# Twelve VectorE operations in other places of a hand-listed order, and seven PSUM tiles in other banks

## The chip, the cores and the metric

One core of one Trainium2 chip. The metric is the device time of one execution in microseconds (us); the number for a kernel is the median of its runs. Before the change: 225.25 us, three runs from 223.98 to 225.33.

## The reference

For x of 2048 rows by 640 columns (bf16) the kernel computes `g * A + (1 - g) * B`. The gate `g` is a sigmoid of a weighted row sum of x. Branch A is a long convolution: `kv = shift(k) * v` with four taps, then a convolution along the 2048 rows with a 2048-long kernel per column, then a product with q (= x).

```python
k_shift = k_shift + k_pad[:, t:t + S, :] * shift_k[:, ks - 1 - t]     # four taps
kv = k_shift * v
y_f = rfft(kv padded) * rfft(ssm_k padded)
a = q * (irfft(y_f)[:S] + kv * ssm_D)
```

Branch B is a mixer: layernorm, a 640x640 matmul and gelu, four column groups of the result shifted by +1, -1, +2 and -2 rows, a second 640x640 matmul and a residual add, then layernorm, 640x1536, gelu, 1536x640 and a residual.

```python
h = gelu(layernorm(x) @ w1)                      # then four groups of 160 columns shifted in rows
x1 = x + shifted(h) @ w2
b = x1 + gelu(layernorm(x1) @ w3) @ w4
```

## The kernel before

The kernel first records 1176 operations (`Prog.op`, `Prog.dma`), each with the memory that it reads and writes, and then issues them in one global order written out by hand, the list `SEQUENCE`. `schedule` follows that list and gives every PSUM tile the bank that the list `PLACES` holds for it. `emit` splits the order by engine (320 operations on TensorE, 299 on ScalarE, 401 on VectorE, 53 on GpSimd, 103 DMAs on SyncE) and puts semaphore waits where the recorded memory use needs them. So an engine runs its own operations strictly in the listed order, and an operation whose input is late holds up all that stand behind it on its engine. A PSUM tile's first matmul also waits for whoever read the earlier tile in the same bank.

Most operations are recorded by a few helpers, so that nearly all of VectorE's rows in the profile have line L646 (`tt`, a tensor_tensor), nearly all of ScalarE's L656 (`act`), nearly all of TensorE's L678 (`mm`) and the DMAs L234 or L237. Operations are told apart by their shapes, their places and their numbers in `SEQUENCE`.

Branch A works on column chunks c = 0 to 4 of 128 columns. For each: `h_*` transforms the convolution kernel, `kv` applies the taps and the product with v (ScalarE scales, VectorE adds), `kv2`, `x_fwd` and `combine` transform kv, `unit` multiplies the two transforms block by block, and `final` transforms back and multiplies by q. The `unit` is the largest VectorE part; it is what the text calls a product unit:

```python
def unit(c):                       # L1003, shortened
    for o0 in (2, 0):              # two halves of the output blocks
        for a in range(o0 + 2):
            for i in range(2):     # acc[i] for a = 0, else the scratch tmp[i]
                tt(tmp[i] if a else acc[i], x[...], HF[:, c, a, i]..., ALU.mult)
            for i in range(2 if a else 0):
                if turn(...): P.dma("pool", acc[i], tmp[i], accum=True)   # an adding DMA
                else: tt(acc[i], acc[i], tmp[i], ALU.add)
        tt(Y[:, :, 0], ...); tt(Y[:, :, 1], ...)          # result back into XF
        scale(Y[0:1, ...])                                # first row, ScalarE or VectorE
```

Some of the additions are thus adding DMAs that GpSimd issues (L237, GpSimd's queue) after VectorE's products; the next product into the same scratch buffer has to wait for the DMA to land. In unit 0 the products 632 and 633 fill acc[0] and acc[1], 634 and 635 fill tmp[0] and tmp[1], 636 adds tmp[0], 637 is the adding DMA of tmp[1] into acc[1], and 639 is the next product into tmp[1]. Unit 3 has the same pattern with DMA 768 and product 770.

Branch B's matmuls are `mm1`, `mm2` (its result is added to x by VectorE, L966), `mm3` (12 groups of 5 matmuls of 128x512 for each quarter of the rows, gelu by ScalarE) and `mm4`. TensorE's list interleaves them with branch A's transforms; the last of `mm4`, operation 977 of tile 14, stands ahead of most of the last `final`s. The `final`s of column group 1 add branch B's result and store.

In `mm1` the fifth column tile goes through a buffer and is copied, 32 partitions at a time, to shifted places of `hT` (line L932, or by DMA); these copies start at odd or even columns.

Of the kernel before, what the change touches and what calls it, by code (L numbers as in the profile page):

```python
# [433 lines left out]
def bass_gated_mix__ssm_conv_h3__mixer_s_mlp__prompt_kernel(  # L434
    nc, A_q, A_k, A_v, A_shift_k, A_ssm_k, A_ssm_D, B_x, B_w1, B_w2, B_w3, B_w4, gate_w, out,
):
    S, D, F = 2048, 640, 1536
# [3 lines left out]
    P = Prog(nc)  # L441
# [27 lines left out]
    def ps(n, cls):  # L469
# [3 lines left out]
    SEQUENCE = [2, 4, 27, 1, 24, 7, 0, 5, 3, 8, 46, 53, 9, 10, 11, 45, 52, 12, 13, 14, 49, 15, 50, 16, 17, 25, 18,  # L473
# [207 lines left out]
    sp = "sp"  # L681
# [233 lines left out]
    def mm1(sc, t0, n, parts=range(5)):  # L915
        xt = chunk_of[0, sc]
        i0 = t0 // 128 % 4
        for ft in parts:
# [5 lines left out]
            else:  # L924
                hx = hxb[t0 // 256 % 2][:, 0:n]
                act(hx, pr, ACTF.Gelu_apprx_tanh)
                for g in range(4):
                    c0, q = 2 + SHIFT[g] + t0, slice(32 * g, 32 * (g + 1))
                    if turn(sc > 0):
                        P.dma(sp, hT[q, 4, c0:c0 + n], hx[q, :], after=[hT[q, 4, c0 - 1:c0]])  # L930
                        continue
# [135 lines left out]
    for sc in range(4):  # L1067
# [8 lines left out]
        else:  # L1076
            n = 256 if sc < 2 else 512
# [72 lines left out]
```

## Time and profile before

| | |
|---|---|
| Median of three runs | 225.25 us (223.98 to 225.33) |
| Profiled execution: span from first to last instruction | 222.3 us |
| The profiled execution's own time | not told beside its span; the median is 2.95 us above the span |
| Granted TensorE clock, mean | 0.993 |
| TensorE busy | 210.2 us (95%) |
| VectorE busy | 211.8 us (95%) |
| ScalarE busy | 193.4 us (87%) |
| Last VectorE operation, by the timeline | ends at 219.55 us |

Engine names in the rows: PE is TensorE's matmuls, PEld its weight loads, DVE is VectorE, ACT is ScalarE, POOL is GpSimd, SP is SyncE. A row of a timeline gives start, length, engine, line, operation, shapes and count, and in brackets the idle time ahead of it and what ended it. Neighbouring operations of one line are merged into one row, under the shape of the first.

### The profile page before, as it was taken

The numbers are of one execution on the slowest core, as the hardware profiler recorded it, in microseconds if no ns is written. First come the engines' busy times: TensorE is split into PE (matmuls) and PEld (weight loads), VectorE is DVE, ScalarE is ACT, GpSimd is POOL, SyncE is SP. The second block draws the span as 40 slices with busy tenths as digits, with TensorE's granted clock in tenths as the row PEclk, the third lists the DMA queues.
The fourth block names the chain that finished last, engine by engine and source line by source line (L and its number), as shares of the span: only waits on it lengthen the run. The fifth ranks groups of instructions, "written<-read, shape, count | busy, mean of one in ns | idle before, by whom it ended". The sixth has DMA issues, their size and how long they took to land.

```text
span 222.3 us, 3842 instructions
## 1 busy us (share of the span) xinstructions
PE 210.2 (95%) x1403; PEld 125.7 (57%) x1410; DVE 211.8 (95%) x417; ACT 193.4 (87%) x324; POOL 53.5 (24%) x57
## 2 busy tenths in 40 slices
PE   5999989799999999999999999999999999999971
PEld 2588755344675444665445575445666444677650
DVE  6999999899999979999999999999998999999994
ACT  2389999799999999899999999999987698666891
POOL 0422303200003300005140003034015416287431
PEclk9999999999999999999999999999999999999997
DMA  5997999999999999939958874599699959979895
GB/s 166 344 299 181 213 208 246 169 253 190 147 361 212 321 226 172 200 78 189 233 108 146 200 153 94 119 174 184 142 226 138 232 77 265 200 100 96 110 161 112
DMA packets 80561, 41.39 MB, mean 186 GB/s; under 512 B 59129, under 2 KB 77086, under 8 KB 80542
## 3 DMA queue, kind: packets, MB, share of 16 engines
q1 hardware_dynamic: 73872, 31.89, 64.9%
q0 software_dynamic: 6496, 9.18, 26.7%
q8 instruction: 11, 0.18, 0.3%
q10 hardware_dynamic: 174, 0.07, 0.1%
q14 instruction: 8, 0.07, 0.1%
HBM read 14.88 MB, written 5.77 MB: 93 GB/s over the span
## 4 chain that ended last, share of the span: by engine, by line
DVE 65%; PE 13%; ACT 11%; DMA 7%; issue 2%; ACTq 0%
DVE arena L646 59%; ACT arena L656 11%; PE PSall L678 10%; DMA arena<-arena 7%; PE PSall L701 3%; DVE arena L651 2%; DVE arena L932 1%; DVE arena L847 1%; DVE arena L966 1%; PE PSall L908 0%; DVE arena L852 0%; DVE arena L698 0%; DVE arena L848 0%; PE PSall L731 0%; DVE arena L689 0%
## 5 line engine op out<-in xcount | busy, mean ns | idle before, releaser
L678 PE MATMUL PSall<-arena 128*128 128x512 bf16 (+5 forms) x1342 | 202.0, 309 | 4.9 <-DVE arena L646 2.2
L646 DVE TENSOR_TENSOR arena<-arena 128x1024 bf16<-128x1024 bf16 (+13 forms) x266 | 173.4, 712 | 4.1 <-DMA arena<-arena 2.7
L678 PEld LDWEIGHTS PSall<-arena 128*128 128x128 bf16 x1349 | 121.4, 98 | 85.1 <-ACT arena L656 6.7
L656 ACT ACTIVATE arena<-PSall 128x512 bf16<-128x512 f32 (+6 forms) x157 | 93.4, 666 | 10.7 <-PE PSall L736 4.9
L656 ACT ACTIVATE arena<-arena 128x640 bf16<-128x640 bf16 (+5 forms) x105 | 90.7, 892 | 4.5 <-DVE arena L646 4.2
L855 POOL TENSOR_TENSOR arena<-arena 128x2 f32<-128x2 f32 (+2 forms) x15 | 17.1, 1145 | 87.6 <-DVE arena L852 71.4
L237 POOL DMA_DIRECT2D out_dram<-arena x24 | 25.5, 1285 | 15.1 <-DVE arena L646 8.9
L656 ACT ACTIVATE arena<-PSall,arena 128x640 bf16<-128x640 f32 (+2 forms) x32 | 20.4, 655 | 8.5 <-PE PSall L678 8.4
L237 POOL DMA_DIRECT2D arena<-arena x14 | 12.4, 882 | 61.1 <-DVE arena L646 61.1
L966 DVE SCALAR_TENSOR_TENSOR arena<-PSall,arena 128x640 bf16<-128x640 f32 x16 | 12.9, 814 | 0.5 <-PE PSall L678 0.5
L651 DVE TENSOR_SCALAR arena<-arena 128x640 bf16<-128x640 bf16 (+6 forms) x37 | 13.2, 376 | 0.1
L847 DVE BATCH_NORM_STATS2 arena<-arena 128x6 f32<-128x320 bf16 x20 | 8.8, 479 | 1.1 <-DMA arena<-in_A_q_dram 1.0
L701 PE MATMUL PSall<-arena 128*128 128x512 bf16 x15 | 6.4, 586 | 2.2 <-DVE arena L698 2.2
L932 DVE TENSOR_SCALAR arena<-arena 32x256 bf16<-32x256 bf16 (+1 forms) x23 | 5.5, 237 | 0.6 <-ACT arena L656 0.3
L656 ACT ACTIVATION_READ_ACCUMULATOR arena<-arena 128x1 f32 x28 | 5.8, 206 | 0.0
L701 PEld LDWEIGHTS PSall<-arena 128*128 128x128 bf16 x15 | 1.9, 136 | 5.0 <-issue 2.8
L908 PE MATMUL PSall<-arena 128*128 128x128 bf16 x40 | 3.4, 220 | 0.1
L852 DVE SCALAR_TENSOR_TENSOR arena<-arena 128x2 f32<-128x2 f32 (+2 forms) x19 | 3.0, 157 | 0.2 <-ACT arena L656 0.2
L908 PEld LDWEIGHTS PSall<-arena 128*128 128x128 bf16 x40 | 2.5, 98 | 0.5 <-DVE arena L651 0.2
L704 ACT ACT_TABLE_LOAD x1 | 1.3, 1283 | 1.3 <-PEq L1135 1.3
L848 DVE BATCH_NORM_AGGREGATE arena<-arena 128x2 f32<-128x12 f32 x10 | 1.8, 199 | 0.0
L966 DVE DVE_READ_ACCUMULATOR arena<-PSall,arena 128x1 f32 x16 | 1.3, 79 | 0.0
(19 smaller groups left out, 2.9 us busy)
## 6 DMA issues: line engine op xcount, KB each, us to landing
arena<-arena POOLq DMA_DIRECT2D x9, 512.0 KB, 6.5
arena<-in_A_ssm_k_dram SPq DMA_DIRECT2D x5, 512.0 KB, 4.2
arena<-in_A_q_dram SPq DMA_DIRECT2D x6, 320.0 KB, 5.7
arena<-in_B_w_dram SPq DMA_DIRECT2D x1, 1920.0 KB, 10.5
out_dram<-arena SPq DMA_DIRECT2D x16, 96.0 KB, 2.9
out_dram<-arena POOLq DMA_DIRECT2D x16, 96.0 KB, 4.7
arena<-in_A_q_dram SPq DMA_DIRECT2D x8, 192.0 KB, 3.3
out_dram<-arena POOLq DMA_DIRECT2D x8, 192.0 KB, 4.2
```

What stands on the lines that cost most here:

```text
L237: fn = lambda e: e.dma_start(out, in_, **kw)
L646: P.op(eng, lambda e: e.tensor_tensor(o, real(a), real(b), op), [a, b], [o], dve_ns(o, [a, b], 2) if eng == "dve" else 500)
L651: P.op(eng, lambda e: e.tensor_scalar(o, real(a), s1, s2, op0=op0, **({} if op1 is None else {"op1": op1})), [a] + aps, [o], dve_ns(o, [a] ...
L656: P.op("act", lambda e: e.activation(real(o), real(a), f, bias=bias, scale=scale, **({"accum_out": accum} if accum is not None else {})), ...
L678: fns.append(lambda e, l=l, r=r, i=i: e.matmul(real(o), l, r, start=(i == 0), stop=(i == last)))
L701: P.op("pe", lambda e: e.matmul(real(pw), warm[:, 0:128], warm[:, 128:640], start=True, stop=True), [warm], [pw], 427.0 if i < 14 else 216.0)
L847: P.op("dve", lambda e, o=o, i=i: e.bn_stats(o, i), [i], [o], 400)
L852: P.op("dve", lambda e: e.scalar_tensor_tensor(o, a, x, b, op0=op0, op1=op1), [a, b] + aps, [o], n_of(o) / 0.96 + 65)
L855: P.op("pool", lambda g: g.tensor_tensor(o, a, e, ALU.pow), [a, e], [o], dur)
L908: P.op("pe", [lambda e, c=c, pb=pb, xn=xn: e.transpose(real(pb)[:, 128 * c:128 * (c + 1)], xn[:, 128 * c:128 * (c + 1)], ident) for c in r ...
L932: P.op("dve", lambda e, o=hT[q, 4, c0:c0 + n], i=hx[q, :]: e.tensor_scalar(o, i, 1.0, None, op0=ALU.mult), [hx[q, :]], [hT[q, 4, c0:c0 + n ...
L966: P.op("dve", lambda e: e.scalar_tensor_tensor(x, real(pr), 1.0, x, op0=ALU.mult, op1=ALU.add, accum_out=st[1, 0][:, t:t + 1]), [pr, x], [ ...
```

## The change

Read by engine, the new `SEQUENCE` leaves the order of TensorE, ScalarE, GpSimd and SyncE as it was. On VectorE twelve operations of 401 stand elsewhere:

| Operation | What it is | Place before | Place now |
|---|---|---|---|
| 633 | unit 0, first half, product into acc[1] | 168 | 159 |
| 389 | combine(1), the second half (subtract) | 204 | 179 |
| 678 | unit 1, second half, product into tmp[1] | 238 | 232 |
| 677 | unit 1, second half, product into tmp[0] | 243 | 238 |
| 693 | h_even(4), the difference | 287 | 278 |
| 701 | kv(4), the first add of shifted taps | 260 | 266 |
| 766 | unit 3, first half, product into tmp[0] | 290 | 288 |
| 770 | unit 3, first half, product into tmp[0] behind DMA 768 | 305 | 307 |
| 814 | unit 4, second half, result Y part 1 | 353 | 356 |
| 815 | unit 4, second half, the first row | 357 | 360 |
| 1166 | last final (group 1, o 0, q 1), the sum | 388 | 383 |
| 1170 | the same final, product with q, first tile | 395 | 389 |

One wait on another engine's queue follows: GpSimd's DMA 637 waits for both products 633 and 635; the later of the two was 633 and is now 635.

VectorE where unit 0 begins, before. L966 rows are `mm2`'s adds (tiles 13, 8 and 11 in the first row, then 15, 12 and 14), the single 128x2048 row is product 632, the 128x2047 row is add 407 of kv(2), and the three 128x2048 rows are products 635, 634 and 633.

```order
L966 SCALAR_TENSOR_TENSOR arena<-PSall,arena 128x640 x3
L852 SCALAR_TENSOR_TENSOR arena<-arena 128x4
L646 TENSOR_TENSOR arena<-arena 128x2048
L966 SCALAR_TENSOR_TENSOR arena<-PSall,arena 128x640
L646 TENSOR_TENSOR arena<-arena 128x2047
L966 SCALAR_TENSOR_TENSOR arena<-PSall,arena 128x640
L852 SCALAR_TENSOR_TENSOR arena<-arena 128x4
L646 TENSOR_TENSOR arena<-arena 128x2048 x3
L966 SCALAR_TENSOR_TENSOR arena<-PSall,arena 128x640
```

The same place now (a line is added ahead, so L966 reads L967):

```order
L967 SCALAR_TENSOR_TENSOR arena<-PSall,arena 128x640 x2
L646 TENSOR_TENSOR arena<-arena 128x2048
L967 SCALAR_TENSOR_TENSOR arena<-PSall,arena 128x640
L852 SCALAR_TENSOR_TENSOR arena<-arena 128x4
L646 TENSOR_TENSOR arena<-arena 128x2048
L967 SCALAR_TENSOR_TENSOR arena<-PSall,arena 128x640
L646 TENSOR_TENSOR arena<-arena 128x2047
L967 SCALAR_TENSOR_TENSOR arena<-PSall,arena 128x640
L852 SCALAR_TENSOR_TENSOR arena<-arena 128x4
L646 TENSOR_TENSOR arena<-arena 128x2048 x2
L967 SCALAR_TENSOR_TENSOR arena<-PSall,arena 128x640
```

Product 633 was the last of the three 128x2048 rows and now stands ahead of the add of mm2(11), operation 564.

VectorE a little later, before: the add 410 of kv(2) (128x2047), kv2(1), the add 411 (128x2046), and the product 639 that waits for DMA 637.

```order
L646 TENSOR_TENSOR arena<-arena 128x1024 x2
L646 TENSOR_TENSOR arena<-arena 128x2047
L646 TENSOR_TENSOR arena<-arena 128x1024
L646 TENSOR_TENSOR arena<-arena 128x2046
L646 TENSOR_TENSOR arena<-arena 128x2048
```

The same place now:

```order
L646 TENSOR_TENSOR arena<-arena 128x1024 x2
L646 TENSOR_TENSOR arena<-arena 128x2047
L646 TENSOR_TENSOR arena<-arena 128x1024
L646 TENSOR_TENSOR arena<-arena 128x3x2x256
L646 TENSOR_TENSOR arena<-arena 128x2046
L646 TENSOR_TENSOR arena<-arena 128x2048
```

The 128x3x2x256 row is 389, which came 25 operations later, ahead of unit 1's product 661.

VectorE at the end of unit 4, before: 812 and 811 (128x1024), 814 (128x2x512), 1103 of a final (128x256), 813, 1104, 815 (one row).

```order
L646 TENSOR_TENSOR arena<-arena 128x1024 x2
L646 TENSOR_TENSOR arena<-arena 128x2x512
L646 TENSOR_TENSOR arena<-arena 128x256
L646 TENSOR_TENSOR arena<-arena 128x2x512
L646 TENSOR_TENSOR arena<-arena 128x256
L651 TENSOR_SCALAR arena<-arena 1x2x2x128
L646 TENSOR_TENSOR arena<-arena 128x384
```

The same place now:

```order
L646 TENSOR_TENSOR arena<-arena 128x1024 x2
L646 TENSOR_TENSOR arena<-arena 128x256
L646 TENSOR_TENSOR arena<-arena 128x2x512
L646 TENSOR_TENSOR arena<-arena 128x256
L646 TENSOR_TENSOR arena<-arena 128x2x512
L646 TENSOR_TENSOR arena<-arena 128x384
L646 TENSOR_TENSOR arena<-arena 128x256
L646 TENSOR_TENSOR arena<-arena 128x384
L651 TENSOR_SCALAR arena<-arena 1x2x2x128
```

1103 and 1104 each move one result ahead of unit 4's, and the first row 815 comes three operations later.

In `PLACES` seven tiles get other banks: tile 66 (x_fwd(1), first quarter) 4 to 6, tiles 123 and 125 (mm4(1), mm4(3)) 4 to 6 and 6 to 4, tile 134 (mm3(1)) 6 to 3, tiles 142, 143 and 148 (mm3(2)) 4 to 6, 2 to 4 and 4 to 2. With them the waits of some matmuls for ScalarE's reads of earlier tiles go to other reads; the one that comes to wait for a later read with the least in hand is 890, the first matmul group of mm3(2), which waited for 870 and now waits for 895.

The third part is in `mm1`: a shifted copy that starts at an odd column now also waits for the copy that wrote the column beside it, and the two memsets at the edges are recorded as two columns wide.

```diff
-    SEQUENCE = [2, 4, 27, 1, 24, 7, 0, 5, 3, 8, 46, 53, ...
+    SEQUENCE = [27, 46, 2, 4, 1, 7, 45, 0, 5, 24, 3, 8, ...
...
-    P.op("dve", lambda e: e.memset(hT[0:32, 4, 2:3], 0.0), [], [hT[0:32, 4, 2:3]], 70)
+    P.op("dve", lambda e: e.memset(hT[0:32, 4, 2:3], 0.0), [], [hT[0:32, 4, 2:4]], 70)
...
-    P.op("dve", lambda e: e.memset(hT[32:64, 4, S + 1:S + 2], 0.0), [], [hT[32:64, 4, S + 1:S + 2]], 70)
+    P.op("dve", lambda e: e.memset(hT[32:64, 4, S + 1:S + 2], 0.0), [], [hT[32:64, 4, S:S + 2]], 70)
...
                     c0, q = 2 + SHIFT[g] + t0, slice(32 * g, 32 * (g + 1))
+                    near = [hT[q, 4, c0 - 1:c0]] if c0 % 2 else []
                     if turn(sc > 0):
-                        P.dma(sp, hT[q, 4, c0:c0 + n], hx[q, :], after=[hT[q, 4, c0 - 1:c0]])
+                        P.dma(sp, hT[q, 4, c0:c0 + n], hx[q, :], after=near)
                         continue
                     P.op("dve", lambda e, o=hT[q, 4, c0:c0 + n], i=hx[q, :]: e.tensor_scalar(o, i, 1.0, None, op0=ALU.mult),
-                         [hx[q, :]], [hT[q, 4, c0:c0 + n]], n / 3.84 + 65)
+                         [hx[q, :], *near], [hT[q, 4, c0:c0 + n]], n / 3.84 + 65)
```

This gives three copies (122, 184 and 185) a wait for an earlier copy on VectorE itself.

More of the change, by code (lines that the diff above doesn't have):

```diff
@@ L471, in ps @@
         return v if n == 1 else v.rearrange("p (b n) -> p b n", b=2)
-    SEQUENCE = [2, 4, 27, 1, 24, 7, 0, 5, 3, 8, 46, 53, 9, 10, 11, 45, 52, 12, 13, 14, 49, 15, 50, 16, 17, 25, 18,
[59 rows of a table removed]
-    PLACES = [2, 4, 7, 0, 4, 5, 6, 1, 2, 1, 3, 4, 2, 3, 3, 4, 2, 6, 7, 2, 0, 4, 5, 7, 6, 2, 6, 1, 0, 7, 4, 1, 6, 0,
[6 rows of a table removed]
+    SEQUENCE = [27, 46, 2, 4, 1, 7, 45, 0, 5, 24, 3, 8, 47, 25, 48, 28, 9, 130, 26, 10, 11, 31, 53, 12, 52, 32, 13,
[59 rows of a table added]
+    PLACES = [2, 4, 7, 0, 4, 5, 6, 1, 2, 1, 3, 4, 2, 3, 3, 4, 2, 6, 7, 2, 0, 4, 5, 7, 6, 2, 6, 1, 0, 7, 4, 1, 6, 0,
[6 rows of a table added]
     ON = ("0000000011111111111111111011011100110100010000101111000000000000011000000000110100000001010010001101"
```

130 rows, old and new, of tables (PLACES, SEQUENCE) are left out of this document.

## The prediction

> **What bounds the kernel now.** I read the busy line of the page first, then the chain of waits in order of time, then the busy time by stage, then the timelines of single engines at the twelve places.
>
> ```profile
> PE 210.2 (95%) x1403; PEld 125.7 (57%) x1410; DVE 211.8 (95%) x417; ACT 193.4 (87%) x324; POOL 53.5 (24%) x57
> ```
>
> TensorE and VectorE are equally busy and ScalarE is not far behind, so the share alone names no bound. The chain (start, length, what):
>
> ```profile
> 67.57 1.23 DVE arena L646
> ...
> 73.33 8.87 DMA arena<-arena
> ...
> 82.22 16.74 DVE arena L646 x25
> ...
> 162.85 7.62 DMA arena<-arena
> ...
> 207.35 1.32 PE PSall L678 x10
> ```
>
> From 67.57 to 207 the chain runs through VectorE and two adding DMAs of unit 0 (8.87 us) and unit 3 (7.62 us). It shows one chain that was late; it does not show how late the next one was. That is read from the stages (length, then busy of PE, PEld, DVE, ACT, POOL, and the granted clock) and from TensorE's matmuls of mm3(0) between 72 and 81.4 us beside the same shape in the whole run:
>
> ```profile
> 60.00:200.00 140.00, 139.43 (x815) 79.53 (x819) 136.28 (x200) 128.75 (x189) 34.66 (x34) 1.00 0.90 181
> 208.00:222.00 14.00, 8.14 (x63) 5.56 (x60) 11.38 (x41) 8.98 (x19) 3.71 (x4) 0.91 0.77 133
> L678 PE MATMUL PSall<-arena 128*128 128x512 bf16 x46 | 10.1, 379 | 0.0
> L678 PE MATMUL PSall<-arena 128*128 128x512 bf16 x413 | 94.1, 379 | 1.8 <-ACT arena L656 1.3
> ```
>
> TensorE is idle for 0.57 of 140 us. A busy TensorE could still be stretched, so I divide: 46 matmuls in 10.1 us are 0.220 us each, and all 413 take 94.1 us, 0.228 each, where one alone shows 379 ns. They overlap and follow each other at one pitch throughout, with the granted clock at 1.00. So **TensorE runs its fixed list without room until 200 us**, beside VectorE's chain and hardly waiting for it. VectorE has 3.72 us idle in the same stretch. Only behind 208 us does TensorE have room (8.14 of 14.00 busy).
>
> **The change part by part.** The sum is made against the profiled span, 222.3 us; the median is 2.95 us above it, and I keep that difference.
>
> Unit 0. VectorE's idle times there and the GpSimd queue:
>
> ```profile
> 64.33 0.82 DVE L966 SCALAR_TENSOR_TENSOR arena<-PSall,arena 128x640 bf16<-128x640 f32 x1 [0.53 <-PE PSall L678]
> 67.57 1.23 DVE L646 TENSOR_TENSOR arena<-arena 128x2047 bf16<-128x2047 bf16 x1 [0.45 <-ACT arena L656]
> 69.53 3.49 DVE L646 TENSOR_TENSOR arena<-arena 128x2048 bf16<-128x2048 bf16 x3
> 72.94 0.81 DVE L966 SCALAR_TENSOR_TENSOR arena<-PSall,arena 128x640 bf16<-128x640 f32 x1
> 82.22 3.29 DVE L646 TENSOR_TENSOR arena<-arena 128x2048 bf16<-128x2048 bf16 x4 [1.38 <-DMA arena<-arena]
> 69.69 1.92 POOL L855 TENSOR_TENSOR arena<-arena 128x4 f32<-128x4 f32 x1 [26.41 <-DVE arena L852]
> 73.33 1.07 POOL L237 DMA_DIRECT2D arena<-arena  x1 [1.72 <-DVE arena L646]
> ```
>
> Three products from 69.53 to 72.94 are 1.14 us apart. 633 now fills the 0.53 and 0.45 us in which VectorE waited for mm2(11) and for ScalarE's scale 405. It pushes 564 by 0.54, and 407 by under 0.2; all behind it up to 635 stays, and from mm2(14)'s add on VectorE is 1.14 earlier. DMA 637 no longer waits for 633 at the end of the three but for 635, first of them, at 70.75. GpSimd is in its power operation until 69.69 + 1.92 = 71.61, so the DMA starts near 71.6, not 73.33: 1.7 us earlier. Whether it lands as much earlier is not shown: it shares the DMA engines with w4's load.
>
> ```profile
> 70.99 0.37 SPq L237 DMA_DIRECT2D arena<-in_B_w_dram  x1
> 79.64 1.21 DVE L646 TENSOR_TENSOR arena<-arena 128x2046 bf16<-128x2046 bf16 x1
> 98.03 0.94 DVE L646 TENSOR_TENSOR arena<-arena 128x1536 bf16<-128x1536 bf16 x1
> ```
>
> With the 8.87 us of before it lands at 80.5; with no gain at 82.2. I take 81.0, nearer to the measured length. 389 (0.94 us, 0.87 with the usual overlap) comes ahead of 411, which then ends at 80.85 - 1.14 + 0.87 = 80.6. So 639 starts near 81.0 instead of 82.22, and where 389 stood, at 98.03, its 0.87 is gone too: **VectorE is about 2.1 us ahead** (0.9 to 2.5 by the two ends).
>
> This lead meets ScalarE next. 463, which scales a tap for kv(3), and 464, the add behind it:
>
> ```profile
> 107.75 0.82 ACT L656 ACTIVATE arena<-PSall,arena 128x640 bf16<-128x640 f32 x1
> 108.50 2.00 ACT L656 ACTIVATE arena<-arena 128x2048 bf16<-128x2048 bf16 x1
> 111.33 1.22 DVE L646 TENSOR_TENSOR arena<-arena 128x2047 bf16<-128x2047 bf16 x1
> ```
>
> ScalarE comes from PSUM reads that TensorE feeds and is free at 108.5 anyhow; 463 ends at 110.50 and 464 starts 0.83 behind it. With some 0.2 us that ScalarE may gain earlier, VectorE keeps about 1.0 us; the rest becomes a new wait at 464. 677, 678, 693 and 766 then only bring ready work ahead of work that would wait for ScalarE or a DMA: nothing gained, nothing lost while that cover holds. Then comes the other DMA wait:
>
> ```profile
> 170.49 5.57 DVE L646 TENSOR_TENSOR arena<-arena 128x2048 bf16<-128x2048 bf16 x9 [0.89 <-DMA arena<-arena]
> ```
>
> DMA 768 starts about 0.9 us earlier, and two sums of 0.27 each fill the hole ahead of 770: the lead grows by up to 0.5, to about 1.4 us.
>
> TensorE decides what this is worth. It waits for VectorE at one place before 200 us (a weight load behind kv2(1), which gates the first quarter of x_fwd(1)), then in the tail:
>
> ```profile
> 90.79 0.87 PEld L678 LDWEIGHTS PSall<-arena 128*128 128x128 bf16 x6 [0.28 <-DVE arena L646]
> 207.35 7.94 PE L678 MATMUL PSall<-arena 128*128 128x256 bf16 x64 [0.33 <-DVE arena L646]
> 215.65 0.28 PE L678 MATMUL PSall<-arena 128*128 128x256 bf16 x1 [0.35 <-DVE arena L646]
> 216.95 0.28 PE L678 MATMUL PSall<-arena 128*128 128x256 bf16 x1 [1.02 <-DVE arena L646]
> 217.69 0.28 PE L678 MATMUL PSall<-arena 128*128 128x256 bf16 x1 [0.46 <-DVE arena L646]
> 206.32 0.89 DVE L646 TENSOR_TENSOR arena<-arena 128x1024 bf16<-128x1024 bf16 x2
> 207.33 12.22 DVE L646 TENSOR_TENSOR arena<-arena 128x384 bf16<-128x384 bf16 x43
> ```
>
> The 0.28 us at 90.79 goes, since VectorE is there over 1 us earlier. At 207.35 TensorE waits for 1104, which ends at 206.32 + 0.89 = 207.21. One product of unit 4 (814) no longer stands ahead of it and VectorE is ahead, so the 0.33 us goes. What is late next is TensorE's own list. The three waits behind 215 are between the last two finals, whose VectorE work stays (43 operations in 12.22 us, 0.28 each): 1166 comes 0.2 us ahead of operations that were waited for, and 1170 parts two dependent operations. I take 0, between -0.3 and +0.2.
>
> The other parts cost nothing by their cover. The three new waits of the edge copies are for VectorE's own copies that ended long before: 122 starts at 19.92, and its copy ends at 18.39 + 0.22.
>
> ```profile
> 18.39 0.22 DVE L932 TENSOR_SCALAR arena<-arena 32x256 bf16<-32x256 bf16 x1
> 19.92 0.22 DVE L932 TENSOR_SCALAR arena<-arena 32x256 bf16<-32x256 bf16 x1
> 139.19 0.60 ACT L656 ACTIVATE arena<-PSall 128x512 bf16<-128x512 f32 x1
> 141.85 2.03 ACT L656 ACTIVATE arena<-arena 128x2048 bf16<-128x2048 bf16 x1
> ```
>
> Of the banks, 890 now waits for the read 895, which ends at 139.79; TensorE gets to 890 at about 140.07. 0.28 us is left, and ScalarE there follows TensorE, not VectorE: 0, and up to 0.3 if ScalarE slips.
>
> Sum: -0.28 - 0.33 = **-0.6 us**, span 221.7, time 225.25 - 0.6 = **224.6 us** (224.0 to 225.1 in this case).
>
> **The rivals.** First, VectorE sets the end. The chain speaks for it, at 65% VectorE: then all four holes count, 0.53 + 0.45 + 1.38 + 0.89 = 3.25 less some 0.9 that stays as waits for the two DMAs and for ScalarE, so 222.9 us (222.3 to 223.9). Against it stands TensorE's 0.57 us of idle time. The Trainium skill, "Perfetto Trace Analysis", section "Identifying the Most-Contended Engine", sides with this rival: it calls matmul busy time a bad measure of headroom, has TensorE judged by its weight loads' busy share, and would have the engine with the highest occupancy worked on first. By that rule, with PEld at 57% and DVE at 95%, VectorE's holes are worth their whole length and the time is this rival's; the 0.220 and 0.228 us per matmul speak against it here. Chance 0.13.
>
> Second, nothing reaches the end: the two TensorE waits are refilled by ScalarE, which is 92% busy from 60 to 200 us (128.75 of 140). Time 225.2, chance 0.2.
>
> Third, slower: add 701 now comes six operations later, and ScalarE's next scale 703 (row at 141.85) waits for it. The six are about 3.4 us of VectorE work; 701 began at 138.49, so without a lead it begins at 141.9, ends at 143.1 and holds ScalarE 1.25 us:
>
> ```profile
> 138.49 1.22 DVE L646 TENSOR_TENSOR arena<-arena 128x2047 bf16<-128x2047 bf16 x1
> ```
>
> PSUM reads for mm3(2) and the first finals stand behind 703 in ScalarE's list, and the matmuls waiting for those banks have about 0.7 us in hand. It decides if VectorE's lead there is under 0.5 us, that is, if DMA 637 lands no earlier, or later. Price 1.25 - 0.7 = 0.55, with the 0.6 not gained: 225.8 us, more if the DMA gets later still. Chance 0.15. I expect a lead of 1.0, so 703 starts some 0.25 later and no matmul waits.
>
> **How the numbers follow.** The forecast has 0.52, the rivals 0.13, 0.2 and 0.15. A measurement here tells about 1% (2.25 us) from no change. Faster by over 1% needs most of the first rival: 0.09. Slower by over 1% needs four times the third's price: 0.04. The rest, 0.87, is within. The range goes from the first rival's 222.9 to just over the third's, 226.0; the runs of before alone spread over 1.35 us.
>
> **What would show it.** Right: no wait of 0.5 us ahead of 564 and 407; DMA 637 issued near 71.6; 639 near 81 with almost no idle time ahead; a new wait of about 1 us for ScalarE at 464, near 110; TensorE as dense between 60 and 200 us as now, with its waits at 90.79 and 207.35 gone; the last VectorE operation near 219.0. Wrong: TensorE's mm4(14) ending more than 0.5 us earlier, which would mean that it had room; a wait of ScalarE near 142 of over 0.5 us, which is the third rival; or 637 taking over 10 us to land.

## The result, and the profile after

| | before | after |
|---|---|---|
| Median, four runs each on the same chip | 225.25 us (223.98 to 225.33) | 239.05 us (238.05 to 239.74) |
| Ratio after to before, 95% interval | | 1.063 (1.059 to 1.066) |
| Profiled execution, span | 222.3 us | 237.6 us (time 239.74) |
| Granted TensorE clock, mean | 0.993 | 0.965 |

The change made the kernel 13.8 us slower; 224.6 was predicted. Wherever the jam described here arises, the runs of one kernel differ among themselves by up to 9.5 us, so for those kernels the median and the range of all four runs are given. Each kernel was traced in one of its runs, and a trace tells of that run alone.

The busy line of the page after:

```profile
PE 210.7 (89%) x1403; PEld 126.2 (53%) x1410; DVE 212.1 (89%) x417; ACT 193.5 (81%) x324; POOL 53.6 (23%) x57
```

The two stretches of after that answer to those shown of before (length, then busy of PE, PEld, DVE, ACT, POOL, the granted clock, the DMA share and GB/s):

```profile
60.00:200.00 140.00, 125.49 (x714) 70.17 (x719) 123.65 (x183) 118.04 (x169) 28.18 (x27) 0.95 0.91 166
208.00:225.00 17.00, 17.00 (x132) 12.60 (x130) 16.39 (x31) 12.80 (x24) 10.13 (x10) 1.00 0.78 85
```

No engine has more work: PE is busy 210.7 us where it was 210.2, DVE 212.1 where it was 211.8. The stretch from 60 to 200 us, in which TensorE was idle for 0.57 us, now holds 14.5 us of idle time. The chain of waits after says where:

```profile
76.23 11.14 DMA arena<-arena
...
92.88 23.22 PE PSall L678 x135
116.15 15.11 PE PSall L678 x91
131.31 34.67 PE PSall L678 x205
165.98 21.38 DMA arena<-arena
187.41 23.70 PE PSall L678 x124
```

From 92.88 to 165.98 the chain runs through TensorE alone, then it steps onto one DMA of 21.38 us, which is 616, the transposing DMA of ln2(12,14) that mm3(3) needs. The first DMA row is 640, the second adding DMA of unit 0. The timeline of VectorE after gives its waits for DMAs, in the brackets:

```profile
83.11 3.62 DVE L646 TENSOR_TENSOR arena<-arena 128x2048 bf16<-128x2048 bf16 x5 [2.24 <-DMA arena<-arena]
87.40 12.34 DVE L646 TENSOR_TENSOR arena<-arena 128x1024 bf16<-128x1024 bf16 x19 [0.67 <-DMA arena<-arena]
176.09 3.36 DVE L646 TENSOR_TENSOR arena<-arena 128x2048 bf16<-128x2048 bf16 x4 [5.30 <-DMA arena<-arena]
187.22 12.65 DVE L646 TENSOR_TENSOR arena<-arena 128x1024 bf16<-128x1024 bf16 x18 [7.77 <-DMA arena<-arena]
```

They are 639 for 637, 642 for 640, 770 for 768 and 775 for 773. TensorE's two waits after:

```profile
92.44 32.76 PE L678 MATMUL PSall<-arena 128*128 128x512 bf16 x188 [1.42 <-DVE arena L646]
187.41 12.95 PE L678 MATMUL PSall<-arena 128*128 128x512 bf16 x53 [12.78 <-DMA arena<-arena]
```

In the kernel before, the matmuls stood still for only 0.05 us at x_fwd(1) (the 0.28 us of the prediction's row is a gap between weight loads), so these two waits make up 14.15 of the 15.2 us by which the span grew. While TensorE waits, its granted clock falls, and it is slower for some microseconds after:

```profile
177.00:187.00 10.00, 0.00 (x0) 0.00 (x0) 2.42 (x4) 0.16 (x1) 0.00 (x0) 0.50 1.17 131
187.00:191.00 4.00, 3.59 (x11) 1.36 (x12) 3.75 (x7) 0.52 (x1) 0.00 (x0) 0.58 0.26 57
191.00:195.00 4.00, 4.00 (x20) 1.83 (x19) 4.00 (x7) 3.44 (x7) 0.87 (x1) 1.00 0.29 40
```

Why 616 is late is read from SyncE's queue. The rows are 709, the loads 1019 and 1030, and 631 with 616; before:

```profile
157.97 1.71 SPq L234 DMA_TRANSPOSE arena<-arena  x1
160.14 1.33 SPq L237 DMA_DIRECT2D arena<-in_A_q_dram  x2
161.53 6.04 SPq L234 DMA_TRANSPOSE arena<-arena  x2
```

After:

```profile
159.83 1.71 SPq L234 DMA_TRANSPOSE arena<-arena  x1
162.00 1.34 SPq L237 DMA_DIRECT2D arena<-in_A_q_dram  x2
163.39 11.53 SPq L234 DMA_TRANSPOSE arena<-arena  x2
```

GpSimd's adding DMAs 768 and 773 after:

```profile
163.57 0.86 POOL L237 DMA_DIRECT2D arena<-arena  x1 [8.57 <-DVE arena L646]
167.23 0.86 POOL L237 DMA_DIRECT2D arena<-arena  x1 [2.79 <-DVE arena L646]
```

709 transposes the result of VectorE's 708. Product 766 now stands ahead of 708, so 709, 1019, 1030 and 631 are issued 1.86 us later: 1.14 is the product's own length, and by the other 0.72 VectorE is late already when it gets there. 631 needs nothing of 708; its own input, from ScalarE's 630, was ready at 156.17 in the kernel before and at 157.65 in this one. GpSimd's adding DMA 768 (162.85 before, 163.57 after) is later by those other 0.72 us only. So 631, issued 1.3 us ahead of 768 before, is now issued 0.18 us ahead of it. The time from issue to landing, the last number of a row, of 631 and 616 before:

```profile
arena<-arena SPq DMA_TRANSPOSE x1, 4.0
arena<-arena SPq DMA_TRANSPOSE x1, 7.5
```

Of 631, 768 and 616 after:

```profile
arena<-arena SPq DMA_TRANSPOSE x1, 15.0
arena<-arena POOLq DMA_DIRECT2D x1, 512.0 KB, 12.5
arena<-arena SPq DMA_TRANSPOSE x1, 21.4
```

In the DMA view of after between 165.9 and 172 us (queue, packets, MB, share of 16 engines) the engines are busy and move little, 69 GB/s:

```profile
DMA packets 893, 0.42 MB, mean 69 GB/s; under 512 B 843, under 2 KB 843, under 8 KB 893
q1 hardware_dynamic: 840, 0.21, 74.9%
q0 software_dynamic: 53, 0.20, 42.3%
```

q1 holds SyncE's packets (a transposing DMA here is 1280 packets of 256 B, 18 ns each when alone), q0 GpSimd's (4096 B, 327 ns each when alone). In the packet records of this stretch 14 of 768's packets take 1.8 to 2.4 us each, most of them at the same time.

### The profile page after: what moved, and what is told of

It reads as the page before. It is cut to its first block, busy times and chain, and to the rows that moved or that the text cites. A ratio compares the mean times of both kernels' runs of the same rounds, so it can differ in the third digit from the quotient of the medians.

```text
span 237.6 us, 3843 instructions
## 1 busy us (share of the span) xinstructions
PE 210.7 (89%) x1403; PEld 126.2 (53%) x1410; DVE 212.1 (89%) x417; ACT 193.5 (81%) x324; POOL 53.6 (23%) x57
## 4 chain that ended last, share of the span: by engine, by line
PE 41%; DVE 27%; DMA 17%; ACT 9%; issue 2%; SPq 1%; ACTq 0%
PE PSall L678 41%; DVE arena L646 19%; DMA arena<-arena 14%; ACT arena L656 9%; DVE arena L967 3%; DMA arena<-in_A_q_dram 3%; DVE arena L651 2%; DVE arena L847 1%; SPq L237 1%; DVE arena L933 1%; DVE arena L848 0%; DVE arena L852 0%; ACTq L379 0%
## 5 line engine op out<-in xcount | busy, mean ns | idle before, releaser
L656 ACT ACTIVATE arena<-PSall 128x512 bf16<-128x512 f32 (+6 forms) x157 | 93.7, 659 | 13.5 <-PE PSall L678 6.8
L967 DVE SCALAR_TENSOR_TENSOR arena<-PSall,arena 128x640 bf16<-128x640 f32 x16 | 12.9, 815 | 0.0
L701 PE MATMUL PSall<-arena 128*128 128x512 bf16 x15 | 5.6, 529 | 2.2 <-DVE arena L698 2.2
L967 DVE DVE_READ_ACCUMULATOR arena<-PSall,arena 128x1 f32 x16 | 1.3, 79 | 0.0
```

The costliest lines, as they stand in the source:

```text
L656: P.op("act", lambda e: e.activation(real(o), real(a), f, bias=bias, scale=scale, **({"accum_out": accum} if accum is not None else {})), ...
L701: P.op("pe", lambda e: e.matmul(real(pw), warm[:, 0:128], warm[:, 128:640], start=True, stop=True), [warm], [pw], 427.0 if i < 14 else 216.0)
L967: P.op("dve", lambda e: e.scalar_tensor_tensor(x, real(pr), 1.0, x, op0=ALU.mult, op1=ALU.add, accum_out=st[1, 0][:, t:t + 1]), [pr, x], [ ...
```

## The experiments

The theory: the 13 us come from transposing DMAs in flight together with adding DMAs, and 766's place is what made them meet. The rivals: the banks or the other eleven moves; a slow path of two transposing DMAs behind one another. The ratio of each experiment is to the kernel before as it was run again beside it (medians from 224.00 to 224.81 us), so it is not the quotient with 225.25.

**Undo 766, keep the rest.**

```diff
-  ... 928, 630, 766, 1001, 980, 707, 929, 718, 708, 762, ...
+  ... 928, 630, 1001, 980, 707, 929, 718, 708, 766, 762, ...
```

> The changed kernel with one of the twelve moves undone: product 766 stands behind 707 and 708 again; the other eleven moves and the seven banks stay. Theory (crossing): 766 ahead of 708 made DMA 709 and the whole SyncE queue behind it later, so that the transposing DMA 631 is issued at the same time as GpSimd's adding DMA 768, and the two together hardly move. Then 709 is issued near 158.7 instead of 159.83, 631 near 162.2, about 1.2 us ahead of 768; 631 lands near 166.5, 616 near 173, and the time is 225 to 227 us. Rival (the rest): the banks or the other eleven moves cost the 13.8 us; then the time stays at 237 to 240 us.

Measured: 224.92 us, 1.000 of before (0.998 to 1.002). 631 and 616 are issued at 161.65 and 165.18 and land 4.0 and 6.7 us later. The seven banks, the edge copies and the other eleven moves together make no difference beyond 0.5 us either way; they were not taken apart.

**Move 766 alone, in the kernel before.**

```diff
-  ... 706, 718, 693, 696, 707, 708, 1010, 1011, 915, 1012, 766, 928, ...
+  ... 706, 718, 693, 696, 766, 707, 708, 1010, 1011, 915, 1012, 928, ...
```

> The kernel before with nothing but product 766 moved ahead of 707 and 708. Theory (crossing): 709 is issued 1.2 us later, near 159.2, 631 near 162.7, within 0.3 us of DMA 768 (162.85); 631 takes over 10 us to land, 616 lands near 185, time 236 to 240 us. Rival (the rest): 225 to 226 us, since the one product of 1.1 us has cover.

Measured: 238.45 us (231.88 to 241.41); the profiled run is the fastest of the four. SyncE's rows of 709 and of 631 with 616 in it:

```profile
158.98 1.75 SPq L234 DMA_TRANSPOSE arena<-arena  x1
162.55 5.89 SPq L234 DMA_TRANSPOSE arena<-arena  x2
```

TensorE's wait for 616 in it:

```profile
179.02 21.22 PE L678 MATMUL PSall<-arena 128*128 128x512 bf16 x101 [5.99 <-DMA arena<-arena]
```

One move of one product is enough. 631 landed at 172.94, 616 at 178.97. The cost is 13.6 us by the median; this fastest run is 7.1 us above the median of before.

**Leave VectorE as changed, take 631 out of the way.**

```diff
-  ... 708, 762, 696, 709, ... 1030, 765, 631, 962, ...
+  ... 708, 762, 696, 631, 709, ... 1030, 765, 962, ...
```

> The changed kernel with only SyncE's order altered: the transposing DMA 631, whose input is ready at 157, is issued ahead of 709 instead of behind 709, 1019 and 1030. VectorE's order and the banks are those of the changed kernel. Theory (crossing): 631 is issued near 158 and lands near 162.5, before 768 is issued at 163.57, so nothing crosses; 709 lands near 164.5 to 165.5, in time for 723 at 167.2; time 225 to 227 us. Rival (the rest): 237 to 240 us. A third way, that any two transposing DMAs in flight at once stall: then 709 and 631 would each take over 6 us here.

Measured: 225.45 us, 1.003 (1.000 to 1.007). 709 is as late as in the changed kernel (159.87), so 709 being late is not what costs. 631 and 709 are in flight one behind the other and each lands 4.3 us after its issue, which speaks against the third way.

**Make 631 late without moving VectorE.** The kernel before, with a wait added, first for 764, then for 765:

```diff
+    for a, b in [(631, 764)]:       # second kernel: (631, 765)
+        P.ops[a].preds.setdefault(b, False)
     sched = P.schedule(SEQUENCE, PLACES)
```

> The kernel before, orders and banks untouched, with one wait added: the transposing DMA 631 also waits for VectorE's product 764 (ends at 162.55), so that it is issued near 162.7 instead of 161.53, that is, together with the adding DMA 768 (162.85). Theory (crossing): 631 lands over 10 us later, 616 is held as in the changed kernel, time 234 to 240 us. Rival (the rest): 1.2 us of delay on a DMA that has 10 us in hand is worth nothing, 225 to 226 us.

Measured: 225.32 us, 1.003 (1.001 to 1.006). The expectation was missed: 631 was issued 0.27 us ahead of 768, nearly as close as with 766 alone moved (0.17), and landed in 6.0 us. By the packet records, when 768's first packet started (165.45) all but 104 of 631's packets had gone, and those passed at once. So the theory was sharpened to the packets still unsent, and the wait put later.

> The kernel before with one added wait: the transposing DMA 631 waits for product 765 (ends at 163.69), so it is issued near 163.9, a microsecond behind the adding DMA 768 (162.9); VectorE's order and the banks are those of before. With the wait for 764 the issue at 162.69 still let all but some 70 of 631's roughly 1280 packets pass ahead of 768's. Theory (crossing, sharpened): what counts is how many transposing packets are still unsent when the adding DMA's 4096-byte packets start near 165; here about half or more are, so the two jam: 631 lands later than 175, time 231 to 240 us. Rival (709 or the loads 1019 and 1030 have to be late as well, as they are wherever 766 was moved): no jam, 225 to 227 us.

Measured: 229.57 us (226.72 to 231.06). Late, but by another pair than expected: 768's packets went first and undisturbed (it landed in 5.1 us), 631 behind them (7.0 us), and it was 616, 1.2 us later than before, that met 773. Among the waits of the profiled run (total, times, longest):

```profile
PE PSall L678 <- DMA arena<-arena: 4.1, 1, 4.1
```

Its DMA view, first 616 from issue to landing, then the two queues from 170.0 to 172.3 us:

```profile
arena<-arena SPq DMA_TRANSPOSE x1, 10.7
...
q0 software_dynamic: 125, 0.40, 88.6%
q1 hardware_dynamic: 145, 0.04, 10.8%
```

125 packets of GpSimd's, nearly all 773's, and 145 of SyncE's. They alternate, 327 ns against 31 ns, so 616 advances at the pace of the adding packets. The Trainium skill, "DMA: Bandwidth & Descriptors", section "Queues, rings and completion order", says that each DMA engine takes turns between the queues that have work, a packet at a time; the trace agrees here. But turns alone do not explain the jam: the 128 packets of one adding DMA are 8 turns on each of 16 engines, by an estimate 8 x 0.327 = 2.6 us, while 631 took 11.0 us longer after the change than before and 616 took 13.9 us longer. In the trace after the change, and in that with 766 alone moved, the extra time holds spells in which 13 and 15 packets of 768 take 1.8 to 4.5 us each at about the same time. What holds them up is not shown.

**Take the partner away.** The changed kernel with the sum of DMA 768 done by VectorE (its digit in `ON`):

```diff
-    ON = ("...0001010010001101"
+    ON = ("...0001010010001100"
```

> The changed kernel, with the sum of DMA 768 done as an addition on VectorE at the same place of the order (one more VectorE operation of 1.2 us, one adding DMA less). 631 and 616 are issued as late as in the changed kernel. Theory (crossing): without its partner 631 lands 4 to 5 us behind its issue, near 168; 616 meets only the adding DMA 773 and lands by 176; time 225.5 to 229 us. Rival (transposing DMAs queued behind one another stall by themselves): 631 still takes over 10 us, time 237 to 241 us.

Measured: 224.30 us, 1.002 (0.999 to 1.004). With 631 and 616 issued later than in the changed kernel (165.16, 167.69) they land in 5.5 and 4.3 us. Two transposing DMAs behind one another do not stall; a partner in q0 is needed.

**Split the two crossings.** The changed kernel with 773 done by VectorE and 768 left as a DMA, and the kernel with 631 behind 765, also with 773 by VectorE:

```diff
-          "00100001010000100010...
+          "00000001010000100010...
```

> The changed kernel with the sum of DMA 773 done by VectorE (one more VectorE operation of 1.2 us); 768 stays an adding DMA. This splits the jam into its two crossings, 631 with 768 and 616 with 773. If each has its own price: 631 is issued with 768 as in the changed kernel and lands at 171 to 178, 616 then meets only the adding stores 889, 883 and 931 and lands at 178 to 183 instead of 187; time 230 to 236 us. If the first crossing carries everything: 238 to 240 us. If the second carries everything: 225 to 228 us.

Measured: 228.97 us (226.25 to 232.94), between the ranges of the first and the third case. 631 still met 768 and took 9.5 us, but 616 landed at 175.02. So, by the medians, 10 of the 13.8 us need the second crossing, 616 with 773 and the stores. The stores are part of it, since GpSimd, freed of 773, issued the first of them at 163.10 instead of 167.76, which the expectation had not counted.

> The kernel before with 631 held behind product 765, as in the run that came to 229.6 us, and with the sum of DMA 773 done by VectorE. There 631 went through behind 768 and landed 7 us after its issue, but 616 met 773 and the stores and landed at 176.8, and TensorE waited 4.1 us. Theory (crossing): without 773, 616 (issued near 166) lands by 174 and the time is 224.5 to 226.5 us. Rival (616 is late only because 631 is late ahead of it in the queue): 616 lands at 176 to 177, time 229 to 231 us.

Measured: 224.98 us, 1.002 (1.000 to 1.004): the 5 us of the kernel with 631 behind 765 are gone. 616 landed at 175.40, later than the 174 expected, 7.1 us after its issue at 168.29.

What the traces of these kernels give, in us (the packets are counted in the trace's packet records):

| Kernel | 631 issued | 768 issued | 631's packets unsent at 768's first, of 1280 | 631 landed | 616 issued | 616 landed | profiled run | median |
|---|---|---|---|---|---|---|---|---|
| before | 161.53 | 162.85 | 37 | 165.50 | 164.96 | 172.42 | | 225.25 |
| 766 back | 161.65 | 162.97 | 47 | 165.63 | 165.18 | 171.85 | 224.60 | 224.92 |
| 631 first | 157.71 | 163.61 | 0 | 162.05 | 165.95 | 174.18 | 225.41 | 225.45 |
| 631 behind 764 | 162.69 | 162.96 | 104 | 168.72 | 165.07 | 174.03 | 224.86 | 225.32 |
| 766 alone | 162.55 | 162.72 | 78 | 172.94 | 164.83 | 178.97 | 231.88 | 238.45 |
| 773 by VectorE | 162.36 | 162.57 | 320 | 171.83 | 164.94 | 175.02 | 226.25 | 228.97 |
| after | 163.39 | 163.57 | 788 | 178.35 | 165.98 | 187.36 | 239.74 | 239.05 |
| 631 behind 765 | 163.18 | 162.31 | 1280 | 170.18 | 166.12 | 176.83 | 229.12 | 229.57 |

In the kernel before, 768's first packet starts when 37 of 1280 are left: the two miss each other by less than half a microsecond. What decides between 78 (jammed) and 104 (not) is open; each count is from one run, while the runs with 766 alone moved go from 231.88 to 241.41 us. That is 5 and 6.5 packets an engine on the mean; how they were spread over the 16 engines the records do not tell.

**The first step by itself.** The kernel before with 633 and 389 moved, nothing else:

```diff
-  ... 621, 564, ... 634, 633, 637, ... 423, 411, ... 821, 389, 450, ...
+  ... 621, 633, 564, ... 634, 637, ... 423, 389, 411, ... 821, 450, ...
```

> The kernel before with only the first two moves, 633 ahead of 564 and 389 ahead of 411; nothing else. The prediction's first step by itself: by it 637 is issued near 71.6, lands near 81.0, VectorE gains 2.1 us at 98, TensorE loses its two waits, time 224.6 us. Rival (the earlier issue meets w4's load): 637 is issued near 71.7 but lands near 83, the load takes about 15.5 us, VectorE idles 1.5 to 2.3 us ahead of 639, TensorE is idle 1 to 2 us between 75 and 120 us, and the time is 225.2 to 226.5 us.

Measured: 224.10 us, 1.000 (0.998 to 1.003). VectorE's two waits, 639 for 637 and 642 for 640, in it:

```profile
81.87 3.62 DVE L646 TENSOR_TENSOR arena<-arena 128x2048 bf16<-128x2048 bf16 x5 [0.97 <-DMA arena<-arena]
86.57 12.34 DVE L646 TENSOR_TENSOR arena<-arena 128x1024 bf16<-128x1024 bf16 x19 [1.08 <-DMA arena<-arena]
```

TensorE at x_fwd(1) in it:

```profile
91.61 33.57 PE L678 MATMUL PSall<-arena 128*128 128x512 bf16 x193 [0.50 <-DVE arena L646]
```

The load of w4 in it, KB and us from issue to landing:

```profile
arena<-in_B_w_dram SPq DMA_DIRECT2D x1, 1920.0 KB, 14.5
```

637 was issued at 71.88 instead of 73.33 and landed at 81.84 instead of 82.20; 640 was issued 0.8 us earlier and landed 1.5 us later, at 86.54, and VectorE waits 1.08 us for it where it did not before. The load took 14.5 us where it took 10.5. Not all of this is the earlier issue: in two kernels that keep the order of before up to 155 us (631 behind 765 with 773 by VectorE, above, and before with 768 by VectorE, below), 640 landed at 87.35 and 86.53, the load took 13.1 and 13.5 us, and TensorE waited 0.88 and 0.83 us at x_fwd(1). The wait there thus changes from one run of the same order to the next.

**Hold the adding DMAs to their old times.** The changed kernel with 766 back, with 637 waiting for 445, then with 640 waiting for 398 as well (in `SEQUENCE` they then stand behind 445 and 398, too):

```diff
+    for a, b in [(637, 445), (640, 398)]:      # first kernel: (637, 445) alone
+        P.ops[a].preds.setdefault(b, False)
```

> The changed kernel with 766 behind 708 again, and with the adding DMA 637 held back by a wait for VectorE's 445, so that it is issued near 73.3 as in the kernel before instead of near 71.9. Theory: issued at 71.3 to 71.9, beside the start of w4's load, 637 took 10.7 to 11.5 us and landed at 82.9 to 83.1, and the load took 15.3 to 15.8 us; issued at 73.1 to 73.5 it took 8.7 to 8.9 and landed at 81.8 to 82.3, and the load 10.5 to 11.1. So holding it makes it land earlier, near 82.0, and 639 follows at once; the load takes about 10.6 us. Time 224.0 to 225.2 us, against 225.2 to 226 if holding it only costs.

Measured: 224.41 us, 1.000 (0.997 to 1.003). 637 landed at 82.25, near the expected 82.0, but the load took 12.5 us, not 10.6, VectorE waited 1.43 us for 637, and 640 landed at 86.47. Neither gain nor cost.

> The changed kernel with 766 behind 708 again and with both adding DMAs of unit 0's first half held to the issue times of before: 637 waits for VectorE's 445 (73.0), 640 for 398 (77.1). With 637 alone held, 637 landed at 82.25 but 640, issued at 76.21, landed at 86.47 against 85.06 in before, and VectorE had a new idle 0.6 us ahead of 642. If an adding DMA issued earlier beside w4's load only lands later, 640 issued near 77.4 lands near 85.2, 642 starts near 86, kv2(1) is 0.6 to 0.9 us ahead of the kernel with one DMA held, TensorE's wait near 91 shrinks to 0.3 us or less, and the time is 223.6 to 224.3 us beside 224.2 for before. If the landing follows the load whatever is done: 640 lands near 86.5 again and the time stays within 0.1% of before.

Measured: 223.35 us, 0.997 (0.994 to 0.9996), the only kernel whose interval lies below 1, by about 0.7 us. Its upper end is at 0.9996, and of this many kernels one may come out so by chance, so a gain is likely at most. Its profiled run, 225.04, is the second slowest of twelve, and 640 landed at 87.10 in it, as if it had not been held; that the gain comes by an earlier landing of 640 is not shown.

**Does VectorE's chain set the time?** The kernel before with 768 done by VectorE, by the same digit of `ON` as above:

> The kernel before with the sum of DMA 768 done by VectorE, nothing else. In before, 616 and 768 meet for a short time (19 of 616's 1280 packets take over 1 us). Without 768, 616 lands by 170 instead of 172.4. If TensorE's own list sets the time, as the prediction read it, this is worth nothing: 224 to 225.5 us, within 0.3% of before, though VectorE has 1.2 us more to do and has lost a wait of 0.9 us. If the chain through VectorE sets it: 0.3 us slower.

Measured: 225.01 us, 1.001 (0.999 to 1.003). 616 landed at 170.31 instead of 172.42. That 2.1 us off this DMA is worth nothing fits a TensorE that did not wait for it. Between the two chains the run cannot decide: VectorE has 1.2 us more to do and 0.9 us less to wait, so its chain would be 0.3 us longer, and the interval, -0.3 to +0.8 us, holds both 0 and 0.3.

The traces say more. In six of them TensorE's matmuls wait at one place only between 60 and 200 us, at x_fwd(1):

| Kernel | wait at x_fwd(1) | span | span less the wait |
|---|---|---|---|
| 633 and 389 alone | 0.50 | 222.06 | 221.56 |
| 766 back, 637 held | 0.53 | 222.26 | 221.73 |
| 766 back | 0.81 | 222.44 | 221.63 |
| 766 back, both held | 1.47 | 222.86 | 221.39 |
| 631 first | 1.78 | 223.26 | 221.48 |
| after, 768 by VectorE | 3.21 | 224.79 | 221.58 |

The last column agrees within 0.35 us, though the last kernel gives VectorE one more operation. The span less VectorE's idle time in the same stretch goes from 219.0 to 219.7 us. This speaks for TensorE's list, lengthened by its own waits, as what sets the time; VectorE and the DMA 640 count where TensorE waits for them, and there in full. With one trace for each kernel it is an argument, not a test.

## Why the prediction was wrong, point by point

- **The bound was probably read rightly, up to the jam.** The six spans above follow TensorE's wait at x_fwd(1). The run that gave VectorE 1.2 us more to do and took 0.9 us of waiting from it came out within 0.3% of before, but it cannot tell the two chains apart.
- **The step that failed is the sentence on 677, 678, 693 and 766, "nothing gained, nothing lost while that cover holds".** It priced 766 as a VectorE operation with other ready work beside it. Behind 766 stood 707 and 708, behind 708 DMA 709, and behind 709 in SyncE's order 631 and 616, which need neither. 766's 1.14 us went onto four DMAs at once, 709, 1019, 1030 and 631. 616 itself was issued no later by it (164.83 with 766 alone moved, 164.96 before); it landed late because 631 and 768 ahead of it, and 773 beside it, moved slowly. 616 had next to nothing in hand: in the kernel with 631 behind 765 TensorE began to wait for it near 172.7 (176.8 less 4.1), and before it landed at 172.42. Moving 766 alone cost 13.6 us, moving it back returned 14.1.
- **None of the rivals was this.** The slower one sat at 701 and 703. With 766 back, ScalarE waits there for 0.33 us and no matmul follows:

```profile
143.03 2.00 ACT L656 ACTIVATE arena<-arena 128x2048 bf16<-128x2048 bf16 x1 [0.33 <-DVE arena L646]
```

- **The landing of 637 was mis-sized, and 640 was left out.** The two holes ahead of 564 and 407 were filled and 637 was issued at 71.85, as predicted. The prediction took 81.0 for an issue near 71.6 and named over 10 us as a sign that it is wrong; after the change it took 11.2. Issued between 71.3 and 71.9 it landed at 80.48, 81.84, 82.71, 82.86 and 83.08 in five kernels; issued between 73.05 and 73.5, at 81.65 to 82.33 in eight. On the mean, 82.2 against 82.0, nothing is won, while the load of w4 beside it takes 14.5 to 15.8 us instead of 10.5 to 13.5. 640 behind it landed at 86.38 to 88.95 in the five and at 84.52 to 87.10 in the eight. So the lead of 2.1 us never came, and 768, predicted 0.9 us earlier, was issued 0.72 us later after the change and 0.12 us later with 766 back.
- **The 0.28 us at 90.79 was not there to be won.** It is a gap between weight loads; the matmuls stood still for 0.05 us. The row for weight loads has a like gap of 0.32 us at 120.45, at which the matmuls lose 0.04, so "one place before 200 us" is misread as well. Instead of going, the matmuls' wait became 0.50 us with 633 and 389 alone and 1.42 us after, of which up to 0.9 also comes without any edit there.
- **The 0.33 us at 207.35 went, but the reason given is not shown.** With 766 back and with 633 and 389 alone, TensorE has no such wait there. It is gone as well in kernels that leave 814 where it was: with 633 and 389 alone, in which VectorE is ahead (busy 137.0 us from 60 to 200 us, 136.3 before), and with 631 behind 764 or 765, in which only TensorE came there later. The sum of the edits without 766 is 0.0 us (-0.5 to 0.5), where -0.6 was predicted.
- **The banks and the edge copies cost nothing that was seen**: with the other eleven moves they stay within 0.5 us of before.

## What to carry to other kernels

An instruction that is moved ahead of another delays what the other issues, and an in-order DMA queue passes that delay to every DMA behind it, needed or not. So list the queue behind each DMA whose producer moves, with how long each landing has in hand, and which DMAs of other queues will then be in flight with it. Put a DMA whose input has long been ready ahead of one that waits for a late producer, and keep transposing DMAs apart from adding DMAs; here two orders of the same DMAs differ by 13.6 us. Whether it is the adding, the 4096-byte packets or GpSimd's queue that the transposing DMAs have to be kept from, no run here tells.

## What the runs showed of the hardware

- A transposing DMA of 256-byte packets and an adding DMA of 4096-byte packets slow each other when they are in flight together. From the first issue to the last landing 631, 768, 616 and 773 took 12.2 us before and 24.0 us after. Alone or nearly so, 631 and 616 land in 3.9 to 5.5 us, and 768 lands in 5.1 to 7.6; together they took 15.0, 21.4 and 12.5 us. In the kernel with 766 alone moved, 15 packets of 768 took 4.2 to 4.5 us each at the same time, while pairs of one adding and one transposing packet still passed one by one.
- A landing can follow some time after the last packet: with 631 behind 764 the last of 631's 1280 packets ended at 166.08 and the DMA landed at 168.72, while 768's packets were still running; before, 165.02 and 165.50.
- An adding DMA issued 1.5 us earlier beside a 1920 KB load landed no earlier on the mean (82.2 against 82.0 us), and the load took 14.5 to 15.8 us instead of 10.5 to 13.5.
- TensorE's granted clock was 0.50 in the stretch from 177 to 187 us in which it waited and 0.58 over the four microseconds after, where 11 of its matmuls were busy for 3.59 us, 0.33 us each against 0.228 in the whole run before.
